# Two loads for the first two row tiles, three for the key weights, and a key product moved ahead of a tile's transposes

## The chip, the cores and the metric

The kernel runs on one core of a Trainium2 chip. The metric is device time in microseconds (us) of one launch; the time before is the median of three runs. A profile of one further execution is read beside it. TensorE does matmuls (PE; its weight loads are PEld), VectorE is DVE, ScalarE is ACT, GpSimd is POOL, and SyncE is SP, which here only issues DMAs; ACT's queue issues a few as well.

## The reference

Two blocks work on the same input x (2048 rows of 512, bf16), and a gate per row mixes them:

```python
x = A_x
g = _sigmoid((x * gate_w).sum(-1, keepdims=True))
a = _A_ref(x, A_wqkv, A_wo)              # linear attention, 32 heads of 16
b = _B_ref(x, B_w1, B_w3, B_w2)          # (silu(x @ w1) * (x @ w3)) @ w2, 1376 wide
return g * a + (1 - g) * b
# _A_ref: q, k, v from x @ wqkv;  phi(t) = where(t > 0, t + 1, exp(t)) + 1e-6
#   kv = sum over rows of phi(k)^T v per head;  z = sum over rows of phi(k)
#   o = (phi(q) @ kv) / (phi(q) . z + 1e-6);  a = o @ wo
```

The key product k = x @ wk comes first, as the sums over all rows are needed before any row's output.

## The kernel before, in words

The 2048 rows are 16 tiles of 128 rows, in four blocks of four tiles. x is held twice on the chip: `x_sb` with rows on the partitions, and `xT` with the 512 columns on the partitions in four chunks (`kc`), which is what the products with weights read. Tiles 2 to 15 of `xT` come from DMAs that transpose (L92, L95); tiles 0 and 1 are transposed on TensorE.

**Loads.** SP issues, in order: the first two tiles of x as one DMA (L85), in which partition p takes rows 2p and 2p+1, so that each row of the DMA is 2 KB; the transposing DMAs of tiles 2 and 3 (L92); then, per block, a transposing DMA (L95) and a plain one of x rows (L100); then the other weights (L101 to L115). ACT issues the key weights `wk_sb` as two halves, chunks 0 and 1 (L86) and 2 and 3 (L87), then loads its function table with a trial activation (L89). As tiles 0 and 1 hold even and odd rows, the two stores of these tiles go through `out_first`, which has the same order.

**Start on TensorE.** `emit_warm` (L166) issues matmuls on constants, which need no DMA: groups of four that each use 32 of the array's columns (`tiled`), and some that use all (`whole`). Their result is not used. Then `emit_xT(t)` (L183) transposes a tile: two transposes into one PSUM tile, copied to `xT` by DVE (chunks 0 and 1, L193), and two more, copied by ACT (chunks 2 and 3, L195). `emit_k_mm` (L197) is one key product: 128 rows, one chunk, 512 output columns; four chunks add up to a tile's k. `emit_k_phi` applies phi and adds to the running sum.

TensorE's order is the program's own (`manual_schedule` of that engine, L158): warm matmuls, tile 0's transposes, tile 1's transposes, then key products. The products of tiles 0 and 1 stand in an order written out by hand (L413), chunk and tile: (0,0), (1,0), (0,1), (1,1), (2,0), (3,0), followed by the rest of tile 1 and tiles 2 and 3. From tile 4 on each tile's key products stand behind `emit_xp` (L216), which multiplies x with phi(k) of an earlier tile. Query products, the feed-forward block and the outputs follow.

Of the kernel before, what the change touches and what calls it, by code (L numbers as in the profile page):

```python
# [17 lines left out]
def kernel(  # L18
# [12 lines left out]
    nc = tc.nc  # L31
    P = nc.NUM_PARTITIONS

    Bb, S, D = A_x.shape
# [5 lines left out]
    TB = 512  # L40
# [11 lines left out]
    x2d = A_x.flatten_outer_dims()  # L52
    out2d = out.flatten_outer_dims()
# [11 lines left out]
    x_sb = consts.tile([P, NT, D], BF16, name="x_sb")  # L65
    xT = consts.tile([P, KC, S], BF16, name="xT")
    wk_sb = consts.tile([P, KC, D], BF16, name="wk_sb")
# [9 lines left out]
    wqkv_r = A_wqkv.rearrange("(kc d) n -> d kc n", d=P)  # L77
# [2 lines left out]
    x_r = x2d.rearrange("(t p) d -> p t d", p=P)  # L80
    dq = nc.sync
    TF = 2
    x_first = x2d[0 : TF * P, :].rearrange("(p j) d -> p j d", j=TF)
    out_first = out2d[0 : TF * P, :].rearrange("(p j) d -> j p d", j=TF)
    dq.dma_start(out=x_sb[:, 0:TF, :], in_=x_first)  # L85
    nc.scalar.dma_start(out=wk_sb[:, 0:2, :], in_=wqkv_r[:, 0:2, D : 2 * D])  # L86
    nc.scalar.dma_start(out=wk_sb[:, 2:4, :], in_=wqkv_r[:, 2:4, D : 2 * D])  # L87
    pre = consts.tile([1, 1], FP32, name="pre")
    nc.scalar.activation(out=pre[:], in_=nc.const_aps.tensor(0.0, [1, 1], FP32), func=ACT.Exp)  # L89
    for t in range(TF, TPB):  # L90
# [3 lines left out]
    for tb in range(1, NTB):  # L94
        dq.dma_start(  # L95
            out=xT[:, :, tb * TB : (tb + 1) * TB], in_=x2d[tb * TB : (tb + 1) * TB, :],
# [7 lines left out]
    with nc.allow_non_contiguous_dma(reason="one gate weight per partition and chunk"):  # L104
        dq.dma_start(
            out=wr_sb[:, :, 2 * FR : NR], in_=gate_w.rearrange("(kc d o) -> d kc o", d=P, o=1)
# [3 lines left out]
    for fsl in (slice(0, FM // 2), slice(FM // 2, FM)):  # L110
# [12 lines left out]
        out=bm, in_=bm, pattern=[[-Dh, HPC], [0, Dh]], compare_op=ALU.is_ge, fill=0.0,  # L123
# [3 lines left out]
        out=bm, in_=bm, pattern=[[Dh, HPC], [0, Dh]], compare_op=ALU.is_ge, fill=0.0,  # L127
# [38 lines left out]
    def emit_warm(tiled, whole):  # L166
        warm = psX.tile([P, TB], FP32, tag="XP3", name="warm")
        for n in tiled:
            for i in range(NG):
                gsl = slice(i * G, (i + 1) * G)  # L170
                nc.tensor.matmul(
                    warm[gsl, 0:n], lhsT=warm_l[:, gsl], rhs=warm_r[:, 0:n], start=True, stop=True
                )
        for n in whole:
            nc.tensor.matmul(
                warm[:, 0:n], lhsT=warm_l, rhs=warm_r[:, 0:n], start=True, stop=True
            )

    emit_warm((TB, TB, TB, TB, TB, TB // 2), (P, P))

    st = {}

    def emit_xT(t):  # L183
        for h in range(2):
            xTp = psX.tile([P, 2, P], BF16, tag=f"XP{(2 * t + h) % 4}", name="xTp")
            for j in range(2):
                kc = 2 * h + j
                nc.tensor.transpose(  # L188
                    out=xTp[:, j, :], in_=x_sb[:, t, kc * P : (kc + 1) * P], identity=ident[:]
                )  # L190
            xT_t = xT[:, 2 * h : 2 * h + 2, t * P : (t + 1) * P]
            if h == 0:
                nc.vector.tensor_copy(out=xT_t, in_=xTp[:])  # L193
            else:
                nc.scalar.activation(out=xT_t, in_=xTp[:], func=ACT.Copy)  # L195

    def emit_k_mm(k_ps, t, kc):  # L197
        nc.tensor.matmul(  # L198
            k_ps[:], lhsT=xT[:, kc, t * P : (t + 1) * P], rhs=wk_sb[:, kc, :],
            start=(kc == 0), stop=(kc == KC - 1),  # L200
        )
# [162 lines left out]
    def emit_out(tb, tt):  # L364
        t = tb * TPB + tt
        tsl = slice(tt * P, (tt + 1) * P)

        if t < NT - 1:
            parts = [(0, D, True)]
        else:  # L370
            h, q7 = D // 2, 7 * D // 8
            parts = [(0, h, True), (h, q7, True), (q7, D, True)]
        if t < NT - 1:
            o_out = work.tile([P, D], BF16, tag="o_out", name="o_out")
        else:
            o_out = consts.tile([P, D], BF16, name="o_last")
        lo = 0
        for i, (a, b, store) in enumerate(parts):
            o_ps = psX.tile([P, b - a], FP32, tag=f"XP{2 + (tt + i) % 2}", name="o_ps")
            for c in range(KC):  # L380
                nc.tensor.matmul(  # L381
                    o_ps[:], lhsT=st[tb, "pqT"][:, c, tsl], rhs=W_sb[:, c, a:b],
                    start=(c == 0), stop=False,
                )
            nc.tensor.matmul(  # L385
                o_ps[:], lhsT=st[tb, "hTr"][:, tsl], rhs=w2r_sb[:, a:b],
                start=False, stop=False,
            )
            for fc in range(FC):
                nc.tensor.matmul(  # L390
                    o_ps[:], lhsT=st[tb, "hT"][:, fc, tsl], rhs=w2_sb[:, fc, a:b],
                    start=False, stop=(fc == FC - 1),
                )
            if i < 2:
                nc.scalar.activation(  # L395
                    out=o_out[:, a:b], in_=o_ps[:], func=ACT.Copy, scale=omg[:, t : t + 1]
                )
            else:
                nc.vector.tensor_scalar(  # L399
                    out=o_out[:, a:b], in0=o_ps[:], scalar1=omg[:, t : t + 1], scalar2=None,  # L400
                    op0=ALU.mult,
                )
            if store:
                rows = out_first[t] if t < TF else out2d[t * P : (t + 1) * P, :]
                eng = nc.scalar if i == 1 else nc.sync
                eng.dma_start(out=rows[:, lo:b], in_=o_out[:, lo:b])
                lo = b


    k0 = [psM.tile([P, D], FP32, tag="mm", name=f"k0_{t}") for t in range(TPB)]  # L410
    emit_xT(0)
    emit_xT(1)
    for kc, t in ((0, 0), (1, 0), (0, 1), (1, 1), (2, 0), (3, 0)):  # L413
        emit_k_mm(k0[t], t, kc)
    emit_k_phi(k0[0], 0)
    for t in range(1, TPB):
# [15 lines left out]
    with tc.manual_schedule(engines={ENG.DVE}):  # L432
# [18 lines left out]
        for dc in range(KC):  # L451
# [9 lines left out]
            out=z_sb[:].rearrange("p (b f) -> p b f", f=Q),  # L461
            in_=z_col[:, :, None].to_broadcast([P, NB, Q]),
# [3 lines left out]
        for c in range(KC):  # L466
# [10 lines left out]
            out=kvT_sb[:], in0=kvT_ps[:],  # L477
# [40 lines left out]
    for tb in range(NTB):  # L518
        for fc in range(FC if tb == 0 else 0, FC):
            emit_ffn(tb, fc)  # L520
        nx = tb + 1
        for tt in range(TPB):
            if nx < NTB:
                emit_q(nx, tt, psX, "XP0")
                if tt % 2 == 0:
                    emit_rem(nx, tt // 2, psX, "XP1")
                    if tt == 2:
                        emit_omg(nx)
            emit_out(tb, tt)
            if nx < NTB:  # L530
                emit_den(nx, tt)
        if nx < NTB:
            emit_norm(nx)
# [30 lines left out]
```

## Time and profile before

| | us |
|---|---|
| median of three runs | 178.9 |
| the three runs | 177.85, 178.94, 178.90 |
| profiled execution | 178.08 |
| its span (first to last instruction) | 176.4 |
| TensorE busy in it | 172.9 (98% of the span) |
| DVE, POOL, ACT busy | 118.1, 67.1, 65.0 |

The span is what the profile's views cover; 1.68 us of the profiled execution lie around it. Times in the views count from the span's start. A matmul's own duration includes its way through the array, so a row of matmuls that follow each other is better read by the distance of their starts. A product of 512 columns has 379 ns as its mean duration, and in the chain of work four of them take 0.86 us.

### The profile page before, as it was taken

What the parts mean: (1) busy time and instruction counts of PE and PEld (TensorE: products, weight loads), DVE (VectorE), ACT (ScalarE), POOL (GpSimd) and SP (SyncE); (2) the same over time, 40 slices, a digit from 0 to 9 for tenths busy, and PEclk for the clock granted to TensorE, in tenths of its full rate; (3) what the DMA queues carried; (4) which work ended last, traced back from release to release, by engine and by line L of the source; (5) the groups of instructions that cost most, each with busy time, mean ns of one, the idle gap of its engine ahead of it and who ended that gap; (6) DMA issues with size and microseconds to landing.
All of it is one profiled execution on the core that took longest, in us unless ns stands there. A gap on an engine that the chain in (4) does not pass through costs nothing.

```text
span 176.4 us, 2653 instructions
## 1 busy us (share of the span) xinstructions
PE 172.9 (98%) x963; PEld 83.1 (47%) x963; DVE 118.1 (67%) x205; ACT 65.0 (37%) x122; POOL 67.1 (38%) x100
## 2 busy tenths in 40 slices
PE   7999999999999999999999999999999999999994
PEld 3444444464445454444454544444545444444463
DVE  0596867899999637597875466977754669776000
ACT  3634224475424333324243333233434323331222
POOL 7297755789009423282003232820032329100000
DMA  5999999921002311143000101240002022300002
GB/s 180 240 207 281 280 361 367 349 71 24 9 4 60 67 37 37 37 61 73 18 0 7 54 24 47 59 82 2 4 7 67 7 66 55 65 4 0 30 30 60
DMA packets 29884, 15.14 MB, mean 86 GB/s; under 512 B 20944, under 2 KB 29232, under 8 KB 29872
## 3 DMA queue, kind: packets, MB, share of 16 engines
q1 hardware_dynamic: 29184, 14.41, 31.1%
q10 hardware_dynamic: 688, 0.57, 1.0%
q8 instruction: 7, 0.11, 0.3%
q14 instruction: 5, 0.04, 0.1%
HBM read 8.42 MB, written 2.10 MB: 60 GB/s over the span
## 4 chain that ended last, share of the span: by engine, by line
PE 96%; DMA 2%; DVE 0%; issue 0%
PE o_ps L390 20%; PE up_ps L348 20%; PE gate_ps L340 19%; PE o_ps L381 8%; PE q_ps L231 8%; PE XP L218 8%; PE k_ps L198 6%; PE r_ps L255 3%; PE k L198 2%; PE o_ps L385 2%; DMA x_sb<-in_A_x_dram 2%; PE xTp L188 1%; PE gate L340 0%; PE kvT_ps L472 0%; PE W_ps L506 0%; DVE o_last L399 0%
## 5 line engine op out<-in xcount | busy, mean ns | idle before, releaser
L348 PE MATMUL up_ps<-xT,w_sb 128*128 128x512 bf16 x160 | 41.1, 379 | 0.0
L340 PE MATMUL gate_ps<-xT,w_sb 128*128 128x512 bf16 x156 | 40.0, 379 | 0.0
L239 POOL TENSOR_TENSOR qz<-pq,z_sb 128x512 f32<-128x512 bf16 x16 | 18.5, 1163 | 52.3 <-DVE pq L153 52.3
L353 ACT ACTIVATE th<-gate_ps 128x512 bf16<-128x512 f32 x39 | 23.3, 597 | 39.3 <-PE gate_ps L340 38.9
L390 PE MATMUL o_ps<-w_sb,hT 128*128 128x512 bf16 (+3 forms) x180 | 37.5, 355 | 0.0
L355 DVE SCALAR_TENSOR_TENSOR gs<-th,gate_ps 128x512 bf16<-128x512 bf16 x39 | 26.6, 683 | 5.5 <-ACT th L353 5.1
L360 DVE TENSOR_TENSOR hT<-up_ps,gs 128x512 bf16<-128x512 f32 x40 | 27.5, 690 | 3.7 <-PE gate_ps L340 0.5
L150 DVE TENSOR_SCALAR phi_m<-phi_e 128x512 bf16<-128x512 bf16 x32 | 13.8, 432 | 20.8 <-ACT phi_e L148 20.7
L308 POOL TENSOR_TENSOR pqn<-pq,rden 128x256 bf16<-128x256 bf16 x32 | 19.1, 628 | 18.0 <-DVE rden L299 15.4
L390 PEld LDWEIGHTS <-hT 128*128 128x128 bf16 x180 | 16.9, 98 | 17.8
L348 PEld LDWEIGHTS <-w_sb 128*128 128x128 bf16 x160 | 15.6, 98 | 18.9
L340 PEld LDWEIGHTS <-w_sb 128*128 128x128 bf16 x159 | 15.4, 98 | 18.6 <-issue 0.2
L395 ACT ACTIVATE o_out<-o_ps,omg 128x512 bf16<-128x512 f32 x15 | 10.3, 687 | 28.8 <-PE o_ps L390 28.8
L208 POOL TENSOR_TENSOR pks<-pks,pk_sb 128x512 f32<-128x512 f32 x15 | 17.4, 1162 | 7.3 <-DVE pk_sb L153 6.7
L381 PE MATMUL o_ps<-W_sb,pqT 128*128 128x512 bf16 (+3 forms) x72 | 16.8, 355 | 0.0
L231 PE MATMUL q_ps<-wq_sb,xT 128*128 128x512 bf16 x64 | 16.4, 379 | 0.0
L218 PE MATMUL XP<-pk_sb,x_sb 128*128 128x512 bf16 x64 | 16.3, 379 | 0.0
L242 DVE TENSOR_REDUCE den<-qz 128x32 f32<-128x512 f32 x16 | 11.0, 685 | 7.9 <-POOL qz L239 7.8
L148 ACT ACTIVATE phi_e<-k_ps 128x512 bf16<-128x512 f32 x12 | 7.2, 597 | 14.4 <-PE k_ps L198 14.4
L148 ACT ACTIVATE phi_e<-q_ps 128x512 bf16<-128x512 f32 x16 | 9.6, 597 | 7.8 <-PE q_ps L231 7.8
L198 PE MATMUL k_ps<-wk_sb,xT 128*128 128x512 bf16 x48 | 12.3, 379 | 0.0
L153 DVE SCALAR_TENSOR_TENSOR pq<-q_ps,phi_m 128x512 bf16<-128x512 f32 x16 | 11.1, 691 | 0.5
(69 smaller groups left out, 120.4 us busy)
## 6 DMA issues: line engine op xcount, KB each, us to landing
w_sb<-in_B_w_dram SPq DMA_DIRECT2D x2, 1280.0 KB, 9.7
out_dram<-o_out SPq DMA_DIRECT2D x15, 128.0 KB, 1.7
w_sb<-in_B_w_dram SPq DMA_DIRECT2D x2, 640.0 KB, 8.2
x_sb<-in_A_x_dram SPq DMA_DIRECT2D x2, 512.0 KB, 4.9
x_sb<-in_A_x_dram SPq DMA_DIRECT2D x1, 768.0 KB, 5.2
wk_sb<-in_A_wqkv_dram ACTq DMA_DIRECT2D x2, 256.0 KB, 3.7
wq_sb<-in_A_wqkv_dram SPq DMA_DIRECT2D x1, 512.0 KB, 5.8
wv_sb<-in_A_wqkv_dram SPq DMA_DIRECT2D x1, 512.0 KB, 5.0
```

The source lines that it names most:

```text
L198: nc.tensor.matmul(k_ps[:], lhsT=xT[:, kc, t * P : (t + 1) * P], rhs=wk_sb[:, kc, :], start=(kc == 0), stop=(kc == KC - 1),)
L218: nc.tensor.matmul(XP_ps[dc][:], lhsT=x_sb[:, t, dc * P : (dc + 1) * P], rhs=pk_sb[:, t, :], start=(t == 0), stop=(t == NT - 1),)
L231: nc.tensor.matmul(q_ps[:], lhsT=xT[:, kc, ts_tok], rhs=wq_sb[:, kc, :], start=(kc == 0), stop=(kc == KC - 1),)
L239: nc.gpsimd.tensor_tensor(out=qz[:], in0=st[tb, "pq"][:, tt, :], in1=z_sb[:], op=ALU.mult)
L308: nc.gpsimd.tensor_tensor(out=pqn[:].rearrange("p (i c e) -> p c i e", i=NG, c=KC)[:, :, :, dsl], in0=st[tb, "pq"][:, tt, :].rearrange("p ...
L340: nc.tensor.matmul(gate_ps[:], lhsT=w1_sb[:, kc, fsl], rhs=xT[:, kc, tok_sl], start=(kc == 0), stop=(kc == KC - 1),)
L348: nc.tensor.matmul(up_ps[:], lhsT=w3_sb[:, kc, fsl], rhs=xT[:, kc, tok_sl], start=(kc == 0), stop=(kc == KC - 1),)
L353: nc.scalar.activation(out=th[:], in_=gate_ps[:], func=ACT.Tanh, scale=0.5)
L355: nc.vector.scalar_tensor_tensor(out=gs[:], in0=th[:], scalar=1.0, in1=gate_ps[:], op0=ALU.add, op1=ALU.mult)
L360: nc.vector.tensor_tensor(out=st[tb, "hT"][:, fc, :], in0=up_ps[:], in1=gs[:], op=ALU.mult)
L381: nc.tensor.matmul(o_ps[:], lhsT=st[tb, "pqT"][:, c, tsl], rhs=W_sb[:, c, a:b], start=(c == 0), stop=False,)
L390: nc.tensor.matmul(o_ps[:], lhsT=st[tb, "hT"][:, fc, tsl], rhs=w2_sb[:, fc, a:b], start=False, stop=(fc == FC - 1),)
```

## The change

Tiles 0 and 1 of x are loaded by two DMAs with one row of x (1 KB) per partition each, in the plain order of rows, and are stored in that order. The key weights come as three DMAs: chunk 0, chunk 1, and chunks 2 and 3 together. One group of four half-width warm matmuls and one whole one are left out. On TensorE the first key product of tile 0 stands between the transposes of tile 0 and those of tile 1; the order of the other products is as it was.

```diff
     TF = 2
-    x_first = x2d[0 : TF * P, :].rearrange("(p j) d -> p j d", j=TF)
-    out_first = out2d[0 : TF * P, :].rearrange("(p j) d -> j p d", j=TF)
-    dq.dma_start(out=x_sb[:, 0:TF, :], in_=x_first)
-    nc.scalar.dma_start(out=wk_sb[:, 0:2, :], in_=wqkv_r[:, 0:2, D : 2 * D])
-    nc.scalar.dma_start(out=wk_sb[:, 2:4, :], in_=wqkv_r[:, 2:4, D : 2 * D])
+    for t in range(TF):
+        dq.dma_start(out=x_sb[:, t, :], in_=x2d[t * P : (t + 1) * P, :])
+    for ksl in (slice(0, 1), slice(1, 2), slice(2, 4)):
+        nc.scalar.dma_start(out=wk_sb[:, ksl, :], in_=wqkv_r[:, ksl, D : 2 * D])
...
-    emit_warm((TB, TB, TB, TB, TB, TB // 2), (P, P))
+    emit_warm((TB, TB, TB, TB, TB), (P,))
...
-                rows = out_first[t] if t < TF else out2d[t * P : (t + 1) * P, :]
+                rows = out2d[t * P : (t + 1) * P, :]
...
     emit_xT(0)
+    emit_k_mm(k0[0], 0, 0)
     emit_xT(1)
-    for kc, t in ((0, 0), (1, 0), (0, 1), (1, 1), (2, 0), (3, 0)):
+    for kc, t in ((1, 0), (0, 1), (1, 1), (2, 0), (3, 0)):
         emit_k_mm(k0[t], t, kc)
```

## The prediction

> **What bounds the kernel now.** I read the page's chain of work that ended last first. Its summary says that TensorE is the chain almost from end to end:
>
> ```profile
> PE 96%; DMA 2%; DVE 0%; issue 0%
> ```
>
> DMA's 2% is a single wait at the start. The chain in order of time shows where (start, length, what):
>
> ```profile
> 0.81 2.90 DMA x_sb<-in_A_x_dram
> 3.71 0.05 issue
> 3.76 1.03 PE xTp L188 x8
> 4.79 3.57 PE k L198 x16
> ```
>
> From 3.76 us to the last matmul at 173.77 us there is no link but TensorE. So whatever moves the key products at the start moves the end by the same amount, if nothing later has to wait; and what does not move them is worth nothing. The change touches only what lies before 8 us (and two stores in mid-kernel). The timeline of that stretch (start, busy time, engine, what, and in brackets the idle time before and its releaser):
>
> ```profile
> 2.51 0.18 PEld L171 LDWEIGHTS <-const-bfloat16-1.0 128*32 128x32 bf16 x4 [0.25 <-issue]
> 3.31 0.39 PE L175 MATMUL warm<-const-bfloat16-1.0 128*128 128x128 bf16 x2
> 3.75 0.77 PEld L188 LDWEIGHTS <-x_sb 128*128 128x128 bf16 x8 [0.31 <-DMA x_sb<-in_A_x_dram]
> ...
> 4.19 0.72 DVE L193 COPY xT<-xTp 128x256 bf16<-128x256 bf16 x2 [4.19 <-PE xTp L188]
> 4.40 0.81 ACT L195 ACTIVATE xT<-xTp 128x256 bf16<-128x256 bf16 x2 [1.08 <-PE xTp L188]
> 4.53 0.20 PEld L198 LDWEIGHTS <-xT 128*128 128x128 bf16 x2
> 4.58 3.78 PE L198 MATMUL k<-wk_sb,xT 128*128 128x512 bf16 x16
> 4.96 2.90 PEld L198 LDWEIGHTS <-xT 128*128 128x128 bf16 x14 [0.23 <-DVE xT L193]
> ```
>
> Two things to see. **The copy latency**: tile 0's first transpose starts at 3.76, the DVE copy of its first half at 4.19, the key product that needs it at 4.59: 0.83 us from transpose to product, and during most of it TensorE does tile 1's four transposes. **The clock**: the five full groups of warm matmuls start 0.42 to 0.43 us apart (1.23, 1.65, 2.08, 2.51) for 512 columns, the transposes 0.107 us apart for 128; the products from 4.97 on stand 0.216 us apart for 512 (0.86 us per four in the chain). So TensorE runs at half rate up to some moment inside the first key product, although the granted clock is given as 1.00:
>
> ```profile
> L198 PE MATMUL k<-wk_sb,xT x5: 379/379/541, 4.6 to 5.6; 128*128 128x512 bf16 x5
> ```
>
> The product of 541 ns is the first: 4.59 to the next at 4.96 is 0.376 us. With 0.427 us for a product at half rate and 0.216 at full, 0.32 us of it were slow: the rate turned at 4.91 us, 4.07 us after the first warm matmul (0.84).
>
> **What the change does, step by step.**
>
> *Tile 0's load.* The rows for a transfer of such a size (KB, us from issue to landing):
>
> ```profile
> out_dram<-o_out SPq DMA_DIRECT2D x15, 128.0 KB, 1.7
> ...
> wk_sb<-in_A_wqkv_dram ACTq DMA_DIRECT2D x2, 256.0 KB, 3.7
> ...
> x_sb<-in_A_x_dram SPq DMA_DIRECT2D x1, 256.0 KB, 2.9
> ```
>
> The load of tile 0 alone is half the bytes in as many rows. Above: 2.9 us, if the number of rows counts. Below: 1.7 us, a store on quiet queues. Between: in the view by stretches the queues moved 326 to 338 GB/s from 2.4 to 3.3 us and then 380, so 128 KB less is 0.35 us less: 2.55 us, landing at 3.36. I take this one, as it is the pair's own row scaled. TensorE then starts at 3.41 instead of 3.76, 0.35 us earlier. [...]
>
> *The warm matmuls* lose four of 256 columns (0.21 us) and one of 128. The fifth group would end at 2.94, its one whole matmul at some 3.2 us. So 3.2 is the earliest start that an earlier landing could bring: start between 3.2 and 3.76, centre 3.41.
>
> *Tile 0's product ahead of tile 1's transposes.* This removes the cover of the copy latency. TensorE's queue is in order: behind the waiting product stand tile 1's four transposes, and behind these tile 1's copies on DVE and ACT and every key product. From a start at 3.41: four transposes to 3.84, then TensorE idles until the copy is in, 3.41 + 0.83 = 4.24. Product 1 at half rate to 4.67. Tile 1's transposes start at 4.67, not right behind tile 0's; they end at about 5.01 (two at half rate, two after the turn at 4.91); tile 1's load, issued at 1.26 and half as large as today's pair, has until then. Product 2 takes 5.01 to 5.22. Product 3 needs tile 1's copy: 4.67 + 0.83 = 5.50. In the kernel before, product 3 starts at 5.18 (4.97 + 0.216). From there on both have the same products in the same order. **Net: +0.32 us**: from the start to product 3 it takes 2.09 us (0.83 + 0.43 + 0.83) instead of 1.42 (3.76 to 5.18), 0.67 more, and the start is 0.35 earlier. The ends: start at 3.2 gives product 3 at 3.2 + 0.83 + 0.43 + 0.83 = 5.29, +0.1; start at 3.76 gives +0.5. Where the rate turns later than product 3, the slow products cover the second stretch: product 3 at 3.41 + 0.83 + 2 x 0.427 + 4 x 0.107 = 5.52 against 4.59 + 2 x 0.427 = 5.44, +0.1, and at best -0.1.
>
> *wk as three loads.* Chunk 0 lands between 3.36 (as tile 0) and 4.37 (as today's first half, 0.81 + 3.6); it is needed at 4.24, so 0 to 0.13 us of wait; I take 0, as half the bytes are in front of it. Chunk 1 is needed at 5.01, later than today's 4.37. The second half lands at 5.10 today; issued one DMA (0.45 us) later, at 5.55; first needed after product 4, at 5.50 + 0.43 = 5.93. Hidden by the products. The added issue pushes ACT's table load (1.83, 1.28 us) and the trial activation to an end at 3.32 + 0.45 = 3.77; ACT's first copy is due at 3.41 + 0.64 = 4.05. Hidden, with 0.28 to spare.
>
> *SP's queue* gets one more issue (0.40 us, 0.45 with its gap) ahead of everything. The trace's landings and the starts of the weight loads that need them: transposed tile 2 lands 5.70, needed 6.26; tile 3 6.21 and 7.13; the next block 8.01 and 8.85; its x rows 10.82 and 11.44; the block after that 12.73 and 15.97. The smallest slack is 0.56 us, more than 0.45, and TensorE itself comes later. Cost 0; no gain, as nothing on SP comes earlier, and, if the shift grows to that of a transpose's issue (1.27 us), 1.27 - 0.56 - 0.32 = 0.4. The two stores of tiles 0 and 1 have the same rows, to other places: nothing.
>
> **The clock against the change.** The same idle stretches stand just ahead of the turn at 4.91. [...] From rows alone: if the 4.07 us count anew from the end of the pause at 4.24, the rate turns at 8.31 instead of 4.91, and 3.4 us at half rate cost 1.7 us.
>
> **Which time it starts from.** The profiled execution took 178.08 us with a span of 176.4 (1.68 around it); the three timed runs 177.85, 178.94, 178.90. So 178.08 is a low one. A spread of 1.1 us is about what a turn of the clock some 2 us later would make (an estimate from the rows above; no second trace shows it). The middle of the four known times is 178.5. On the profiled execution the sum is 178.08 + 0.32 = 178.4; on one near 178.9, 178.9 + 0.1 = 179.0. For a median of new runs I take the middle of both kinds, 178.5 + 0.3 = **178.8 us**.
>
> **Rivals.**
> 1. *The clock turns later* (slower): one mechanism, at the idle 3.84 to 4.24; it decides if the half rate then lasts to about 8.3 us. 178.4 + 1.7 = 180.1 from the profiled execution, 180.7 from the slower runs. For it: the gap lies in the 4 us ahead of the turn. Against it: the kernel before also has an idle 0.25 us (3.50 to 3.76) there, and turned. 22%.
> 2. *SP's queue is late*: tile 2's transposed load, or the x rows at 11.44, hold TensorE up: up to 0.4 more, 178.8 to 179.3. Against it the slacks. 10%.
> 3. *The earlier start wins* (faster): tile 0 lands by 3.1 and the turn comes late, so that the idle is covered: -0.1, 177.8 to 178.8. More than the 0.35 to 0.55 us of earlier start can't be won, and that only if the copy latency shrank. 8%.
> 4. Forecast: a loss of 0.1 to 0.5: 178.1 to 179.4. 60%.
>
> The range leaves out the upper part of rival 1 and the lowest runs: **178.1 to 180.4**. About 1% is what a measurement of this kernel can tell from no change, 1.8 us: only rival 1 on slower runs, or a loss of another kind, gets beyond it: slower 20%; faster 4%, by a spread of the runs; within it 76%.
>
> **What the profile after would show.** Tile 0's first transpose at 3.2 to 3.5; an idle of some 0.4 us on the weight loads of the key line, released by the DVE copy, and a second one of up to 0.3 before product 3; product 3 at about 5.5; no other idle of TensorE. Wrong would be: products 0.427 us apart beyond 5.5 (the clock), tile 0 landing at 3.7 or below 3.1, or a wait of TensorE for a DMA after 6 us.

## The result, and the profile after

The change makes the kernel slower. Over 22 executions each, the median goes from 178.33 to 180.19 us; the ratio is 1.0093, with a 95% interval of 1.0074 to 1.0112. The executions also spread more: 177.71 to 178.94 us before, 178.63 to 181.18 after. The profiled execution of the changed kernel took 180.34 us (span 178.6) where that of the kernel before took 178.08 (span 176.4): 2.26 us more.

The chain of work that ended last, of the changed kernel, from its start (start, length, what). Lines are one less than before for most names: L187 is a transpose, L192 the DVE copy, L197 a key product.

```profile
0.81 2.84 DMA x_sb<-in_A_x_dram
3.65 0.05 issue
3.69 0.41 PE xTp L187 x2
4.10 0.02 issue
4.12 0.30 DVE xT L192
4.42 0.05 issue
4.47 0.61 PE k L197
5.08 0.43 PE xTp L187 x4
5.50 4.76 PE k L197 x15
```

Three things are to be seen. Tile 0 lands at 3.65 us, 0.06 earlier than the pair of tiles did. The DVE copy now stands in the chain, as nothing on TensorE covers it. And the last 15 key products take 4.76 us here, where 16 took 3.57. TensorE's weight loads in the timeline tell why (the bracket holds the idle time before and its releaser):

```profile
3.69 0.34 PEld L187 LDWEIGHTS <-x_sb 128*128 128x128 bf16 x4 [0.49 <-DMA x_sb<-in_A_x_dram]
4.47 0.10 PEld L197 LDWEIGHTS <-xT 128*128 128x128 bf16 x1 [0.44 <-DVE xT L192]
...
5.67 0.20 PEld L197 LDWEIGHTS <-xT 128*128 128x128 bf16 x2 [0.33 <-DVE xT L192]
6.15 0.15 PEld L197 LDWEIGHTS <-xT 128*128 128x128 bf16 x1 [0.28 <-ACT xT L194]
6.58 0.15 PEld L197 LDWEIGHTS <-xT 128*128 128x128 bf16 x1 [0.28 <-issue]
...
8.29 0.15 PEld L197 LDWEIGHTS <-xT 128*128 128x128 bf16 x1 [0.28 <-issue]
8.60 0.31 PEld L197 LDWEIGHTS <-xT 128*128 128x128 bf16 x2 [0.16 <-issue]
```

From 5.72 to 8.28 us each key product starts 0.427 us behind the last: half rate. The turn, the moment at which the spacing changes to full rate, is at 8.47 us by this spacing. This trace's own record of the granted clock begins there too, at 8.47. The trace of the kernel before has no such record, so its 4.91 us comes from the spacing alone. The first XP product, which follows the 16 key products, before (first fence) and after (second fence):

```profile
8.20 1.03 PE L218 MATMUL XP<-pk_sb,x_sb 128*128 128x512 bf16 x4
```

```profile
10.11 1.03 PE L217 MATMUL XP<-pk_sb,x_sb 128*128 128x512 bf16 x4
```

So the 2.26 us between the two profiled executions are: **0.54** up to key product 3 (5.18 to 5.72 us), **1.36** from there to the first XP product (3.02 us before, 4.38 after, all of it the half rate), and **0.35** behind the last matmul: from its start to the end of the span it is 2.81 us before and 3.16 after. Between the first XP product and the last matmul the two traces agree to 0.01 us (165.36 and 165.37).

The last part is seen in SP's own waits at the end. Before (first fence) and after (second fence), the wait for the last stores:

```profile
SPq L559 <- DMA out_dram<-o_last: 0.7, 1, 0.7
SPq L559 <- PEq L559: 0.6, 2, 0.4
```

```profile
SPq L559 <- DMA out_dram<-o_last: 1.0, 1, 1.0
...
SPq L559 <- PEq L559: 0.8, 2, 0.6
```

In both traces SP closes the program with a row of five waits, two semaphores each, and the DMAs (72 before, 74 after) are dealt out over eight semaphores in turn. Before, the last store's semaphore was in the last wait, and the others were done while it was out; with two DMAs more it is in the second, and three waits of 0.06 us and what follows come behind it. That is about half of the 0.35; the rest is ACT's last drain, which starts 2.81 us after the last matmul instead of 2.37 (further down).

### The profile page after: what moved, and what is told of

Read it like the earlier page. It is cut to its first block, busy times and chain, and to the rows that moved or that the text cites. A ratio compares the mean times of both kernels' runs of the same rounds, so it can differ in the third digit from the quotient of the medians.

```text
span 178.6 us, 2645 instructions
## 1 busy us (share of the span) xinstructions
PE 174.3 (98%) x958; PEld 83.2 (47%) x958; DVE 118.7 (66%) x205; ACT 64.9 (36%) x122; POOL 66.9 (37%) x100
## 4 chain that ended last, share of the span: by engine, by line
PE 96%; DMA 2%; DVE 0%; issue 0%
PE o_ps L389 19%; PE up_ps L347 19%; PE gate_ps L339 19%; PE o_ps L380 8%; PE XP L217 8%; PE q_ps L230 8%; PE k_ps L197 6%; PE k L197 3%; PE r_ps L254 3%; PE o_ps L384 2%; DMA x_sb<-in_A_x_dram 2%; PE xTp L187 0%; PE gate L339 0%; PE kvT_ps L472 0%; PE W_ps L506 0%; DVE xT L192 0%
## 5 line engine op out<-in xcount | busy, mean ns | idle before, releaser
L197 PE MATMUL k_ps<-wk_sb,xT 128*128 128x512 bf16 x48 | 12.3, 379 | 0.0
```

The lines of the kernel that those rows point to most:

```text
L197: nc.tensor.matmul(k_ps[:], lhsT=xT[:, kc, t * P : (t + 1) * P], rhs=wk_sb[:, kc, :], start=(kc == 0), stop=(kc == KC - 1),)
```

## The experiments

Fourteen kernels ran. The first four change the kernel before, or the changed kernel. The others carry names with "plain": their transposing DMAs are replaced by plain ones of the same bytes. They leave the transposition out, so their results are not the reference's; a control of the same kind shows what that does to the time. "Over before" is the median less the median of the kernel before, measured beside it on the same chip. "The clock theory" in the expectations is that idle TensorE ahead of the turn delays it.

### The three parts alone, and a filler

Order alone:

```diff
     emit_xT(0)
+    emit_k_mm(k0[0], 0, 0)
     emit_xT(1)
-    for kc, t in ((0, 0), (1, 0), (0, 1), (1, 1), (2, 0), (3, 0)):
+    for kc, t in ((1, 0), (0, 1), (1, 1), (2, 0), (3, 0)):
```

> The kernel before with only the order changed: tile 0's first key product ahead of tile 1's transposes; loads and warm matmuls as before. Clock theory (idle TensorE in the 4 us ahead of the turn delays the turn to full rate): an idle of 0.4 us at 4.2 to 4.6 us is added, so the turn comes later in many executions: median 1 to 2 us above the kernel before. Order-only theory (the copy latency lies open, the clock is as before): product 3 moves from 5.18 to 5.7, the median rises by 0.3 to 0.5 us and the spread of the runs stays near 1.2 us.

Measured: median 178.48 us, 0.28 over before; ratio 1.0008 (0.9987 to 1.0029). The median's difference lies inside the interval, but the profile shows the cost: product 3 started at 5.66 us instead of 5.18, 0.48 later, as the order-only theory gave. Full rate was reached during tile 1's transposes, at about 5.0 us by their spacing, so the turn was hardly delayed, and the median is not 1 to 2 us higher, as the clock theory had it for this part alone.

Loads alone:

```diff
-    dq.dma_start(out=x_sb[:, 0:TF, :], in_=x_first)
-    nc.scalar.dma_start(out=wk_sb[:, 0:2, :], ...)
-    nc.scalar.dma_start(out=wk_sb[:, 2:4, :], ...)
+    for t in range(TF):
+        dq.dma_start(out=x_sb[:, t, :], in_=x2d[t * P : (t + 1) * P, :])
+    for ksl in (slice(0, 1), slice(1, 2), slice(2, 4)):
+        nc.scalar.dma_start(out=wk_sb[:, ksl, :], in_=wqkv_r[:, ksl, D : 2 * D])
...
-                rows = out_first[t] if t < TF else out2d[t * P : (t + 1) * P, :]
+                rows = out2d[t * P : (t + 1) * P, :]
```

> The kernel before with only the loads (and stores of tiles 0 and 1) of the change: two loads of 128 KB for x, three for wk; order and warm matmuls as before. In the profile after, tile 0 landed at 3.65 us and tile 1 at 4.24. Clock theory: an idle of 0.1 us ahead of tile 1's transposes is all that is added: within 0.3 us of the kernel before. Theory that the loads themselves cost (SP's queue 0.45 us late, the wk loads late): a TensorE wait for a DMA after 5 us and 0.5 us or more above the kernel before.

Measured: median 179.07 us, 0.87 over before; ratio 1.0032 (1.0014 to 1.0051). Wk's second half landed at 5.90 us instead of 5.10, and product 5, which needs it, started at 5.95, 0.07 after TensorE was free for it; the stretch behind the last matmul had grown by 0.35 us. So the loads do cost, most clearly at the end. The first XP product came 0.33 us later (8.53): besides that wait, the rate turned at 5.46 us in this execution instead of 4.91, worth 0.27, and a wait of 0.20 for tile 1 took back what the earlier start had won. How much of the later turn is the loads' doing is not shown, as the turn varies for the kernel before too (below). This execution, of 178.77 us, was the fastest of twelve, so what the others lose beyond it no trace shows.

Warm matmuls alone:

```diff
-    emit_warm((TB, TB, TB, TB, TB, TB // 2), (P, P))
+    emit_warm((TB, TB, TB, TB, TB), (P,))
```

> The kernel before with only the warm matmuls cut (five groups of four and one whole). Tile 0 still lands at 3.71 us, so TensorE idles from 3.2 to 3.76 instead of 3.5 to 3.76 and nothing else moves. Clock theory: 0.3 us less activity ahead of the turn delays it in some executions: median 0.3 to 1.2 us higher. Order-only theory: no difference, within 0.2 us.

Measured: median 178.58 us, 0.38 over before; ratio 1.0010 (0.9987 to 1.0033). This is no clear difference: the effect, if any, is at the lower end of what the clock theory gave.

The changed kernel with TensorE's idle stretch behind tile 0's transposes filled:

```diff
     emit_xT(0)
+    emit_warm((), (P, P, P))
     emit_k_mm(k0[0], 0, 0)
```

> The changed kernel with three whole warm matmuls of 128 columns (0.107 us each at half rate) between tile 0's transposes and its first key product, where TensorE idled from 4.10 to 4.47 us. Clock theory: the turn comes earlier again, median 0.7 to 1.5 us below the changed kernel, so 0.3 to 1.1 us above the kernel before. Order-only theory: the matmuls lie in idle time, no difference from the changed kernel (1.86 us above the kernel before); if they delay the product, up to 0.1 us more.

Measured: median 179.34 us, 1.14 over before; ratio 1.0056 (1.0036 to 1.0076). That is 0.7 us less than the changed kernel's 1.86, for matmuls whose result is never used, and the spread was 1.0 us (178.89 to 179.90, 12 executions) instead of 2.55 (22 executions). The turn in its profile is at 5.90 us. The chain of work of this run holds a further thing, the transposed load of tile 2:

```profile
1.74 5.52 DMA xT<-in_A_x_dram
7.26 0.05 issue
7.31 1.90 PE k L197 x8
```

It landed at 7.26 us and the product that needs it waited 0.22 us: a load of SP's queue did hold TensorE up here. It was issued 0.48 us later than in the kernel before, and was 5.52 us in flight instead of 4.43. In the changed kernel's profile it landed at 6.54, long before its product at 8.59.

Alone, the parts cost 0.28 + 0.87 + 0.38 = 1.53 us; together 1.86. The clock theory wants the two idle stretches to work together, and this asks for the order and the shorter warm-up without the loads.

### Order and warm-up together, and the same with a filler

Control: all 37 transposing DMAs replaced.

```diff
-        dq.dma_start(out=xT[:, :, tsl], in_=x2d[tsl, :], transpose=True)
+        dq.dma_start(out=xT[:, :, tsl], in_=x2d[tsl, :].rearrange("p (k c) -> p k c", k=KC))
...
-            out=xT[:, :, tb * TB : (tb + 1) * TB], in_=x2d[tb * TB : (tb + 1) * TB, :],
-            transpose=True,
+            out=xT[:, :, tb * TB : (tb + 1) * TB],
+            in_=x2d[tb * TB : (tb + 1) * TB, :].rearrange("(k p) d -> p k d", p=P),
... the same for hTr and pqT
```

> Control for the runs that follow. The kernel before in which all 37 transposing DMAs are plain DMAs of the same bytes into the same places; the transposition itself is left out, so its output is not the reference's. TensorE's work, order, warm matmuls and the first loads are those of the kernel before. All theories: 177.7 to 178.5 us, product 3 near 5.2 us, and the closing 2.8 us after the last matmul, as in the kernel before; if the transposing DMAs slowed the start, a little less.

Measured: median 177.93 us, 0.08 under before; ratio 0.9998 (0.9977 to 1.0019). The control stands for the kernel before. By luck its profiled execution, of 179.03 us, is one of the slower ones. Its timeline of TensorE beside that of the run c4_plain_sp2 (told below; the same start, profiled execution 177.95 us), the second fence:

```profile
3.73 1.03 PE L188 MATMUL xTp<-ident,x_sb 128*128 128x128 bf16 x8
4.56 4.76 PE L198 MATMUL k<-wk_sb,xT 128*128 128x512 bf16 x16
```

```profile
3.75 0.63 PE L188 MATMUL xTp<-ident,x_sb 128*128 128x128 bf16 x8
4.43 3.63 PE L198 MATMUL k<-wk_sb,xT 128*128 128x512 bf16 x16
```

The same instructions, in the same order and without a wait, take 4.76 us or 3.63. The records of the granted clock have the turn at 6.86 and at 3.80 us. So the same start turns early in one execution and 3 us later in another. From the kernel before to the control, the turn is 1.95 us later and the first XP product 0.95 (8.20 and 9.15): half of the delay.

Whole change, on the control:

> The whole change on the control with plain DMAs (transposition left out in both). If the change's cost lies in the clock, the order and the end, and not in how transposing DMAs meet the wk loads: 1.4 to 2.1 us above the control, a spread over 2 us, and the end 0.35 us longer after the last matmul (2.8 to 3.15 us). If transposing DMAs ahead of wk's second half are most of it: under 1 us above the control.

Measured: median 179.50 us in 5 executions, 1.49 over before; ratio 1.0077 (1.0050 to 1.0105). So the change is slow without the transposing DMAs too. But the time is made up otherwise in this profile: wk's second half landed at 6.65 us and product 5 started at 6.69, after a wait of 0.53; the end took 3.14 us; and the turn was at about 5.9 us by the spacing, not at 8.5. The spread over 2 us that was expected did not appear (179.49 to 179.85), in five executions. So this run does not show the delayed turn; the next one does.

Order and warm-up, without the loads, on the control:

> The control with plain DMAs (transposition left out) with the change's order and its cut of the warm matmuls; loads as before. On the kernel before the two alone gave 0.3 and 0.4 us. If costs simply add: 0.7 us above the control. Clock theory (idle of 0.55 and 0.4 us add up ahead of the turn and push it to 8 us and more in many executions): 1.0 to 1.9 us above the control, some runs more than 2 us above its fastest, and no change in the 2.8 us after the last matmul.

Measured: median 180.45 us in 5 executions, **2.44 over before**, where the sum of the two alone is 0.66; ratio 1.0121 (1.0088 to 1.0154). Its profile was the fastest of the five (179.56 us) and has the turn at 7.31. Tile 0 landed at 3.89 us in it, 0.18 later than in the kernel before. The idle stretches stand one behind the other:

```profile
3.93 0.34 PEld L188 LDWEIGHTS <-x_sb 128*128 128x128 bf16 x4 [0.73 <-DMA x_sb<-in_A_x_dram]
4.71 0.10 PEld L198 LDWEIGHTS <-xT 128*128 128x128 bf16 x1 [0.44 <-DVE xT L193]
```

The same with the filler:

```diff
     emit_xT(0)
+    emit_warm((), (P, P, P))
     emit_k_mm(k0[0], 0, 0)
```

> The run c2_plain_orderwarm (order and warm matmuls of the change, plain DMAs, transposition left out; 2.5 us above its control) with three whole warm matmuls of 128 columns between tile 0's transposes and its first key product, in the stretch of 0.4 us in which TensorE idled. Clock theory: the turn comes at 5 to 6 us in most executions, 0.4 to 1.2 us above the control instead of 2.5. If the idle was harmless and the order itself costs 2.5 us: no difference, 180.3 to 180.6.

Measured: median 178.59 us, 0.46 over before; ratio 1.0027 (1.0002 to 1.0052). So three matmuls of no use take off nearly 2 us, from 2.44 over before to 0.46. In its profile the turn comes within tile 1's transposes, at about 5.1 us by their spacing, and the products from 5.67 us on are at full rate:

```profile
4.06 0.36 PEld L175 LDWEIGHTS <-const-bfloat16-1.0 128*128 128x128 bf16 x3
4.54 0.10 PEld L198 LDWEIGHTS <-xT 128*128 128x128 bf16 x1
...
5.67 2.71 PEld L198 LDWEIGHTS <-xT 128*128 128x128 bf16 x14 [0.39 <-DVE xT L193]
```

The two waits of the new order are still there; only the emptiness of the first is gone. This pair of runs shows the cause: the idle time ahead of the turn, and not the order or the wait as such. Ten of the twelve executions lie between 178.18 and 178.95 us; two (179.43 and 180.38) were slow in spite of the filler, and neither was traced.

### What the clock costs by itself, and an attempt at a better start

One group of warm matmuls, order and loads as before:

```diff
-    emit_warm((TB, TB, TB, TB, TB, TB // 2), (P, P))
+    emit_warm((TB,), ())
```

> The control with plain DMAs (transposition left out) with one group of four warm matmuls instead of five and a half and none of the whole ones: TensorE idles from 1.3 to 3.76 us. Order and loads as before. It prices the clock alone. Clock theory: the turn moves from 4.9 us to 4 us after tile 0's first transpose, 7.8, or later; 2.9 us at half rate cost 1.4: 1.0 to 2.0 us above the control, with the turn seen in the spacing of the key products. If the clock's state hangs on something other than TensorE's activity: no difference.

Measured: median 179.65 us, 1.64 over before; ratio 1.0081 (1.0055 to 1.0108). The time is as the clock theory gave. Its profile is that of the fastest execution (178.91 us); the turn is at 6.61 us there, later than 4.91 but not at the 7.8 that the theory named, and no slower execution was traced. The idle stretch in it:

```profile
3.73 1.03 PE L188 MATMUL xTp<-ident,x_sb 128*128 128x128 bf16 x8 [2.26 <-DMA x_sb<-in_A_x_dram]
```

The other way, three more whole warm matmuls, up to tile 0's landing:

```diff
-    emit_warm((TB, TB, TB, TB, TB, TB // 2), (P, P))
+    emit_warm((TB, TB, TB, TB, TB, TB // 2), (P, P, P, P, P))
```

> The control with plain DMAs (transposition left out) with three more whole warm matmuls (0.107 us each), which fill the 0.25 to 0.3 us in which TensorE waited for tile 0. The control and the kernel before show two kinds of executions, near 177.9 and near 178.9. Clock theory: fewer late turns, so fewer executions near 178.9 and a median of 177.8 to 178.0; at most 0.1 us lost where tile 0 has landed first. If that idle does not matter: the same mixture, a quarter or more near 178.9.

Measured: median 178.13 us, the same as before; ratio 0.9998 (0.9979 to 1.0017), 177.85 to 178.95. It gains nothing that can be measured, where the clock theory had a median of 177.8 to 178.0: 0.25 us of idle time by itself does not matter at this start. In the profile the filler ran past tile 0's landing (3.69 us) and the transposes started at 3.83, 0.07 later than before. No version was found that beats the kernel before.

### The loads and the end

Two more DMAs on SP far from the start:

```diff
-    for fsl in (slice(0, FM // 2), slice(FM // 2, FM)):
+    for fsl in (slice(0, FM // 4), slice(FM // 4, FM // 2), slice(FM // 2, 3 * FM // 4), slice(3 * FM // 4, FM)):
```

> The control with plain DMAs (transposition left out) with w3 loaded in four pieces instead of two: two more DMAs on SP, at 23 us, far from the start, so that the eight DMA semaphores are dealt out two places on, as in the change; ACT's queue as before. What the last matmul is followed by took 2.8 us before and 3.15 with the changed loads. Theory that the place of the last store's semaphore among SP's closing waits makes it longer: 2.95 to 3.0 us from the last matmul to the end (0.17 more: three waits behind the one that ends last). Theory that it is ACT's additional DMA alone: 2.8 us.

Measured: 2.97 us from the last matmul to the end, within what the semaphore theory gave. The median, 178.56 us, is 0.43 over before with a ratio of 1.0020 (0.9999 to 1.0040); with early and late turns mixed, 0.17 us are read from the trace and not from the median.

One more DMA on ACT, wk's second half as two single chunks:

> The control with plain DMAs (transposition left out) with wk's second half as two loads of one chunk each: one more DMA on ACT, the semaphores one place on; the first half, x, order and warm matmuls as before. ACT theory of the end: ACT's last drain starts 0.25 to 0.35 us late, as with the changed loads, the end grows by about 0.2 to 0.3 us. Semaphore theory: with one place on, the last store is among the first waits too, 0.1 to 0.2 us. Key products: no wait for wk, as its pieces are issued behind the same first half.

Measured: 3.08 us to the end. ACT's last drain starts 2.75 us after the last matmul instead of 2.36, so both theories hold a part: the place of the semaphore and ACT's late drain. What makes ACT late after one more DMA the traces do not show. The last expectation was wrong: wk's last chunk landed at 5.68 us and its product waited 0.18 us. Median 178.51, 0.38 over before; ratio 1.0019 (1.0001 to 1.0038).

Which of the two loads makes wk late? wk in three, x as one:

> The control with plain DMAs (transposition left out) with only wk in three loads (chunk 0, chunk 1, second half); x tiles 0 and 1 as one load. Theory that wk's own third issue makes its second half late: it is issued at 1.73 instead of 1.30 us, behind the load of tile 2 on SP, and lands at 6.0 us or later instead of 5.3; its first product waits 0.2 us or more; end 0.28 longer (one DMA more, on ACT): 0.4 to 0.9 us above the control. Theory that the second x load does it: the second half lands by 5.6, nothing waits, 0.3 us above the control, all of it at the end.

Measured: median 179.28 us, 1.06 over before; ratio 1.0043 (1.0020 to 1.0066). Its chain of work goes through the third wk load and its issue:

```profile
1.73 4.13 DMA wk_sb<-in_A_wqkv_dram
5.87 0.04 issue
5.91 2.75 PE k L198 x12
```

x in two, wk in two halves:

> The control with plain DMAs (transposition left out) with only x tiles 0 and 1 as two loads; wk in two halves, order and warm matmuls as before. Theory that wk's third issue makes its second half late: the second half lands by 5.5 us, nothing waits for it, 0.1 us above the control from the closing waits. Theory that the second x load does it: landing at 6.0 or later and a wait of 0.2 us or more ahead of the product that needs it.

Measured: median 178.36 us, 0.14 over before; ratio 1.0008 (0.9987 to 1.0029). The second half landed at 5.11 us, nothing waited for it, and the end took 2.92 us. TensorE did wait 0.48 us for tile 1's load, after a start 0.25 us earlier than in the kernel before. So the third wk issue is what makes wk late: 0.44 us later on ACT's queue in c9_plain_wk3 than in the control (1.73 instead of 1.29), the second half landed 0.6 us later (5.87 instead of 5.28), 4.13 us after its issue instead of 3.99. Of the 1.06 us of c9_plain_wk3, its trace shows 0.25 of waiting and 0.28 at the end. The rest, about 0.5, is not accounted for by them; an idle stretch more ahead of the turn would do it, but no late execution of this run was traced.

## Why the prediction was wrong

The time lies in the range, but the likeliest case, a loss of 0.1 to 0.5 us and no measurable change, is not what happened. The first rival was, which had 22%.

*The start.* The step that tile 0 would land after 2.55 us by its bytes is wrong: 2.84 us in the profile, and 2.70 in the run with the loads alone. The upper bound, that the number of rows counts, was the nearer one. The start came 0.06 us earlier, not 0.35.

*The order.* The path from the start to product 3, worked out as 2.09 us, measured 2.03 (3.69 to 5.72), and the two stretches of idle TensorE were there. With the true start this gives 0.54 us in place of 0.32. In the run with the order alone, where the turn was hardly delayed, product 3 was 0.48 late. This step stands. One number in it does not follow: with a start at 3.76 the same three terms give 5.85, 0.67 late, and not 0.5; the 0.48 of that run, which started at 3.79, is close to it because the rate turned within tile 1's transposes.

*The clock.* This is the step that failed: the sum kept the turn at 4.91 us and put its delay at nothing. The rival had named the delay and its price (from 4.91 to 8.31, 1.7 us; measured 8.47, and 1.36 us of it behind product 3), but it was taken for unlikely on the argument that the kernel before also idles for 0.25 us ahead of its turn and turned all the same. That argument is about one idle stretch; the change adds to it twice, 0.25 to 0.48 us ahead of tile 0 and 0.37 behind its transposes. The runs show that the order alone (0.28 us) and the shorter warm-up alone (0.38) cost little and that both together do not (2.44), which no sum over parts gives. The rival also laid the delay to the pause behind tile 0's transposes alone, and the run with the order alone has that pause and turned at about 5.0 us. That 8.31 came so near 8.47 is luck: counting 4.07 us anew from the end of the pause would put the turn of c2_plain_orderwarm at 8.78, and it came at 7.31.

*wk as three loads.* "Hidden by the products" failed. The second half was reckoned to land at 5.55 us, 0.45 later than before; it landed at 6.11 in the changed kernel, hidden by the slow products, and at 5.90 with the loads alone, where product 5 waited 0.07 us; the control with three wk loads waited 0.25, and with the whole change 0.53. The reckoning moved the landing by the load's later issue alone, but it was also longer in flight, 4.38 us in the changed kernel instead of 3.80. What lengthens the flight no run separates.

*SP's queue.* Its smallest slack was given as 0.56 us and its cost as none. In the changed kernel's profile nothing waited; in the run with the filler tile 2's load held TensorE up by 0.22 us. The second rival was half right.

*The end.* A term was missing. The prediction said that the start moves the end by the same amount and looked for waits up to the last matmul only; 0.35 us lie behind it.

*The size.* The reckoning of the spread from the clock was right, and is now seen in a trace: 179.03 us with the turn at 6.86, against 178.08 at 4.91. The median of 178.5 taken for the kernel before was 178.33 over 22 executions. And far less than 1% can be told apart here: over 22 executions each the interval is 0.2% to either side.

## What to carry to other kernels

Count TensorE's idle time ahead of the moment at which the spacing of its matmuls changes to full rate as one sum over all its places: stretches that were nearly free one by one here (0.28 and 0.38 us over before) kept the half rate for microseconds together (2.44 us over before, the turn at 7.31 us instead of 4.91). Matmuls of no use that filled one of them paid there (0.7 and 2 us here), and gained nothing where a short stretch stood alone (178.13 us, the same as before). Where one profile shows that moment close behind an idle stretch, do not take it as fixed; the same start had it at 3.80 us in one execution here and at 6.86 in another, so compare medians of many. And a DMA more is not only its issue: the load behind it can land later than its later issue accounts for (0.6 us for 0.44 in c9_plain_wk3), and the program's last store can move to another place among the closing waits (2.97 us to the end with two DMAs more on SP, 2.81 before).

## What the runs showed of the hardware

The half rate ends at a moment that varies for one and the same start: 3.80, 4.41, 4.91 and 6.86 us in the four traces with an unchanged warm-up and order and x as one load and wk's first half as one (4.91 is worked out from the spacing, the others are records), a spread of 3.06 us. From 4.91 to 6.86 us the first XP product moves by half the delay; from 3.80 to 4.91 it moves by 0.30 of 1.11, as TensorE at the early full rate waits 0.21 us for the copy of tile 0 ahead of product 1. In the changed kernel's trace the record has the full rate from 8.47 us on for 170.67 us, to behind the end of the span at 178.6.

Of the traces of the kernel before (turn at 4.91 us), the order alone (about 5.0), the changed kernel (8.47), the changed kernel with the filler (5.90), and, on the control, order and warm-up (7.31) and these with the filler (about 5.1), two have the turn after 6 us: those with both idle stretches and without the filler. The late turn of c0_plain (6.86) is of another kind: its transposes started at 3.73 us, 0.03 earlier than in the kernel before, and no run shows why its half rate lasted longer. How much idle time it takes to delay the turn no run shows either.

The first load of 128 rows of 1 KB landed 2.41 to 2.84 us after its issue in the five traces that have it (2.70 to 2.84 in the three with the transposing DMAs), one of 128 rows of 2 KB after 2.82 to 3.09: how much half the bytes saved at the start of the program changed from run to run. The end of the program was longer with more DMAs: 2.80 to 2.81 us from the start of the last matmul, 2.92 with one more on SP, 2.97 with two, 3.08 with one on ACT, 3.14 to 3.17 with one on each.
